# Linear attention and an MLP mixer on one core: fp32 dummy matmuls, halves in one product, and a later place for q's transposes

## Chip, cores and metric

The kernel runs on one core of a Trainium2 chip. The metric is the device time of one execution in microseconds, as the median over runs. All ratios are computed as the mean time of one kernel's fast runs over the mean of the other's fast runs of the same rounds, so they are not quite the ratio of the medians quoted beside them. The 95% interval of a ratio stands in brackets.

## The reference

```python
def _attn_ref(q, k, v):                    # 8 batches, 8 heads, 576 rows, head size 64
    phi = lambda x: np.where(x > 0, x, np.exp(x) - 1.0) + 1.0
    q_p, k_p = phi(q), phi(k)
    kv = np.einsum('bhsd,bhse->bhde', k_p, v)
    z = np.sum(k_p, axis=2)
    num = np.einsum('bhsd,bhde->bhse', q_p, kv)
    den = np.einsum('bhsd,bhd->bhs', q_p, z)[..., None] + 1e-06
    return num / den
# the heads side by side give x: 8 x 576 x 512
def _moe_ref(x, w_tok1, w_tok2, w_ch1, w_ch2):
    h = np.maximum(x.transpose(0, 2, 1) @ w_tok1, 0.0) @ w_tok2
    u = x + h.transpose(0, 2, 1)
    return u + np.maximum(u @ w_ch1, 0.0) @ w_ch2
```

## The kernel before: the parts that matter here

The instructions of each engine stand in program order. Batch 0 is done by itself in the opening, about the first 25 us; every later batch is prepared beside the channel matmuls of the one before. In the opening the order on TensorE is: dummies; the transposes of batch 0's first half of q; the column sums of k; two more dummies; the first kv product; the second half's transposes; the numerators; the second kv; then the first token product, 20 matmuls that stand in the profile as L427.

phi(k) is kept as a sum of two terms, kr = max(k, 0) and kp = min(exp(k), 1), so every kv product has two terms.

```python
    def kv_first(c, copy):
        ps = sm_tile()[:, :, 0:2 * D]
        for k_ in (kr, kp):
            for t in range(T):
                on, off = k_ is kr and t == 0, k_ is kp and t == T - 1
                if c == 0:                                   # halves: 2 matmuls of 64x128 by 128 columns
                    for a in range(2):
                        nc.tensor.matmul(out=ps[:, a], lhsT=k_[half[a], c, t],
                                         rhs=v0[half[a], 2 * c:2 * c + 2, t], start=on, stop=off)
                else:                                        # quarters: 4 matmuls of 64x64 by 64 columns
                    for a, i in QUARTERS:
                        nc.tensor.matmul(out=ps[half[i], a, 0:D], lhsT=k_[half[a], c, t, i],
                                         rhs=v0[half[a], 2 * c + i, t], start=on, stop=off)
        ...                                                  # two copies into kvbd

    def warm(m):                                             # dummies: 128x512 bf16
        ps = bank()
        for _ in range(m):
            nc.tensor.matmul(out=ps, lhsT=identity, rhs=identity[:, None, :].to_broadcast([128, 4, 128]),
                             start=True, stop=True)

    def tick(m):                                             # dummies of one column
        ps = sm_tile()
        for k_ in range(m):
            a, i = QUARTERS[k_ % 4]
            nc.tensor.matmul(out=ps[half[i], a, 0:1], lhsT=identity[half[a], 0:64],
                             rhs=identity[half[a], 0:1], start=True, stop=True)
    ...                                                      # cut: loads and memsets
    nc.gpsimd.memset(w1t, 0.0)
    nc.gpsimd.memset(qT[0], 0.0)
    nc.vector.memset(qT[1], 0.0)
    for c in range(2):
        load_v0(c)                                           # v of batch 0, issued by GpSimd
    ...
    for m in (100, 52, 52):
        tick(m)
        warm(4)
    k_first(0, 1)
    ...                                                      # cut
    warm(2)
    kv_first(0, act)
    ...
    # batch 1's q transposes ("qt0", "qt1") and products, by the index of the big group they follow;
    # groups 3 to 11 are mm3 (w_ch1), from 12 on they are blocks of four matmuls on w_ch2
    at0 = {"qt0": 11, "qt1": 13, "vc": 13, "kv": 14, "nd00": 15, ...}
```

## Time and profile before

| | before |
|---|---|
| median of 3 runs | 265.81 us (265.56 to 266.7) |
| span of the profiled run | 264.0 us |
| TensorE busy | 256.9 us, 97% |
| TensorE's first real work | 9.68 us |
| first kv product starts | 11.96 us |
| start of the 36 matmuls that carry on without a break at w_ch1 | 26.48 us |
| idle before batch 1's q transposes | 0.5 us |

In the order of time a row gives the start and the length in us, the engine, the source line, the operation, what it wrote and read, how many instructions were merged, and in brackets the idle time before it with what ended it ("issue" means that nothing the profile shows was waited for). In the chain that ended last a piece has only start, length, engine, tile, line and count. The lines themselves are in the prediction below.

### The profile page before, as it was taken

How to read it: one execution, taken by the hardware profiler on the slowest of the kernel's cores; microseconds unless marked ns; L12 is line 12 of the kernel's file. 1: busy time of each engine (PE TensorE's matmuls, PEld its weight loads, DVE VectorE, ACT ScalarE, POOL GpSimd, SP SyncE). 2: the span in 40 equal slices, each digit the busy share in tenths (PEclk: the TensorE clock that was granted, in tenths of full speed). 3: DMA queues.
4: the chain of work that ended last, by engine and by line, in shares of the span. 5: the costliest groups of instructions: out<-in, count | busy, mean ns of one | idle time of the engine just before them, and what ended most of it. 6: DMA issues, size and time to landing. Idle time of an engine off the chain costs nothing.

```text
span 264.0 us, 5626 instructions
## 1 busy us (share of the span) xinstructions
PE 256.9 (97%) x2344; PEld 136.0 (52%) x2344; DVE 158.6 (60%) x312; ACT 133.0 (50%) x204; POOL 33.5 (13%) x54
## 2 busy tenths in 40 slices
PE   7999999999999999999999999999999999999994
PEld 4685445554744454455554554455554554444642
DVE  5755977967829786948684286938684272420122
ACT  4564878268455358425870358435870354027300
POOL 9730300020002300030001300030001300000000
PEclk9999999999999999999999999999999999999999
DMA  7999999499505996599999991671066500740043
GB/s 252 251 203 274 376 220 391 155 197 370 206 2 113 190 337 266 121 248 386 271 402 178 261 405 65 147 163 42 2 130 120 120 1 2 148 110 0 2 99 100
DMA packets 50089, 48.37 MB, mean 183 GB/s; under 512 B 30288, under 2 KB 35536, under 8 KB 50064
## 3 DMA queue, kind: packets, MB, share of 16 engines
q1 hardware_dynamic: 41904, 35.53, 45.7%
q0 software_dynamic: 7440, 11.44, 20.9%
q10 hardware_dynamic: 720, 1.05, 1.3%
q8 instruction: 18, 0.29, 0.4%
q14 instruction: 7, 0.06, 0.1%
HBM read 35.85 MB, written 9.44 MB: 172 GB/s over the span
## 4 chain that ended last, share of the span: by engine, by line
PE 95%; ACT 1%; DVE 1%; issue 1%; POOL 0%; ACTq 0%; POOLq 0%
PE h_ps L515 33%; PE c_ps L489 32%; PE a_ps L248 6%; PE h_ps L261 5%; PE c_ps L503 4%; PE nd_ps L210 3%; PE bank L573 2%; PE kv_ps L169 2%; PE bank L581 1%; PE h_ps L552 1%; PE bank L427 1%; PE bank L180 1%; PE bank L438 1%; PE bank L392 1%; DVE u L440 0%
## 5 line engine op out<-in xcount | busy, mean ns | idle before, releaser
L496 ACT ACTIVATE cr<-c_ps 128x512 bf16<-128x512 f32 x91 | 53.4, 599 | 76.4 <-PE c_ps L489 76.2
L489 PE MATMUL c_ps<-uT,wc 128*128 128x512 bf16 x384 | 91.5, 379 | 0.0
L515 PE MATMUL h_ps<-wc,cr 128*128 128x512 bf16 x372 | 84.9, 379 | 0.0
L515 PEld LDWEIGHTS <-cr 128*128 128x128 bf16 x372 | 36.0, 98 | 41.3
L489 PEld LDWEIGHTS <-wc 128*128 128x128 bf16 x384 | 35.7, 98 | 36.4 <-issue 0.9
L532 DVE TENSOR_TENSOR o_sb<-h_ps,u 128x512 f32<-128x512 f32 x31 | 21.1, 689 | 23.1 <-PE h_ps L515 23.0
L537 POOL DMA_DIRECT2D out_dram<-o_sb x24 | 14.9, 626 | 153.5 <-DVE o_sb L532 153.5
L222 DVE TENSOR_TENSOR x<-nd_ps,den 128x512 bf16<-128x512 f32 (+1 forms) x42 | 25.3, 603 | 1.5
L139 DVE TENSOR_SCALAR e<-e 128x1152 bf16<-128x1152 bf16 x30 | 13.9, 464 | 12.6 <-ACT e L125 12.5
L273 DVE TENSOR_TENSOR u<-h_ps,x 128x1024 bf16<-128x1024 f32 x12 | 14.3, 1219 | 10.1 <-PE h_ps L261 10.1
L125 ACT ACTIVATE e<-k_raw 128x1152 bf16<-128x1152 f32 x16 | 18.7, 1169 | 2.5 <-DMA k_raw<-in_k_dram 2.5
L125 ACT ACTIVATE e<-q_raw 128x1152 bf16<-128x1152 f32 x16 | 18.4, 1160 | 1.8 <-DMA q_raw<-in_q_dram 1.8
L219 DVE TENSOR_SCALAR den<-nd_ps 128x8 f32<-128x8 f32 (+1 forms) x42 | 6.9, 164 | 18.6 <-PE nd_ps L210 17.9
L210 PEld LDWEIGHTS <-qT 128*128 128x128 bf16 x140 | 11.4, 98 | 9.3 <-issue 0.2
L261 PE MATMUL h_ps<-ar,w2p 128*128 128x512 bf16 x60 | 16.0, 379 | 0.1
L210 PE MATMUL nd_ps<-kvbd,qT 128*128 128x130 bf16 x140 | 15.1, 223 | 0.0
L251 ACT ACTIVATE ar<-a_ps 128x512 bf16<-128x512 f32 x14 | 7.6, 594 | 13.7 <-PE a_ps L248 13.7
L248 PE MATMUL a_ps<-x,w 128*128 128x512 bf16 x56 | 14.4, 379 | 0.0
L542 DVE TENSOR_TENSOR o_sb<-h_ps,ut 128x512 f32<-128x512 f32 x4 | 2.8, 689 | 18.7 <-PE h_ps L515 18.7
L151 ACT CAST vs<-v_raw 128x1152 bf16<-128x1152 f32 x12 | 13.9, 1159 | 0.0
L131 DVE TENSOR_SCALAR y<-q_raw 128x1152 bf16<-128x1152 f32 x16 | 12.4, 775 | 0.6 <-DMA q_raw<-in_q_dram 0.3
L140 DVE TENSOR_TENSOR qp<-e,y 128x1152 bf16<-128x1152 bf16 x16 | 12.1, 758 | 0.6
(112 smaller groups left out, 226.4 us busy)
## 6 DMA issues: line engine op xcount, KB each, us to landing
k_raw<-in_k_dram SPq DMA_DIRECT2D x16, 576.0 KB, 9.0
q_raw<-in_q_dram SPq DMA_DIRECT2D x16, 576.0 KB, 7.8
v_raw<-in_v_dram SPq DMA_DIRECT2D x14, 576.0 KB, 11.0
out_dram<-o_sb POOLq DMA_DIRECT2D x24, 256.0 KB, 4.6
wc<-in_moe_w_ch_dram POOLq DMA_DIRECT2D x8, 384.0 KB, 9.7
out_dram<-o_sb SPq DMA_DIRECT2D x9, 128.0 KB, 2.3
out_dram<-o_sb ACTq DMA_DIRECT2D x7, 128.0 KB, 2.6
out_dram<-o_sb POOLq DMA_DIRECT2D x6, 128.0 KB, 5.9
```

What stands on the lines that cost most here:

```text
L125: nc.scalar.activation(out=e, in_=f, func=AF.Exp)
L139: nc.vector.tensor_scalar(out=e, in0=e, scalar1=1.0, scalar2=None, op0=ALU.min)
L210: nc.tensor.matmul(out=o[:, a], lhsT=qT[b][:, t0:t0 + 128], rhs=kvbd[b][:, c, a], start=True, stop=True)
L222: nc.vector.tensor_tensor(out=x[b][:, rs[0]:rs[0] + m, HG * D * g:HG * D * (g + 1)].rearrange("p r (h d) -> p r h d", h=HG), in0=v_[:, :, ...
L248: nc.tensor.matmul(out=ps[:, mt], lhsT=w1t[:, b, ms] if r == R else w1[:, r, ms], rhs=x[b][:, r, :], start=(r == 0), stop=(r == R))
L261: nc.tensor.matmul(out=ps[:, i], lhsT=w2v(kt, r, b), rhs=ar[b][:, kt, :], start=(kt == 0), stop=(kt == NT - 1 and not add))
L273: nc.vector.tensor_tensor(out=u[b][:, rs[0]:rs[0] + m], in0=ps[:, 0:m], in1=x[b][:, rs[0]:rs[0] + m], op=ALU.add)
L489: nc.tensor.matmul(out=ps, lhsT=wc1[:, kj, 128 * mc:128 * mc + 128], rhs=uT[b][:, :, kj], start=(kj == 0), stop=(kj == NDM - 1))
L496: nc.scalar.activation(out=cr[b][:, mc, :], in_=ps, func=AF.Relu)
L515: nc.tensor.matmul(out=ps, lhsT=crt[:, kc, :] if t == 8 else cr[b][:, kc, 128 * r:128 * r + 128], rhs=wc2[:, kc, :], start=(kc == 0), stop ...
L532: nc.vector.tensor_tensor(out=o, in0=ps, in1=u[b][:, r, :], op=ALU.add)
L537: (nc.scalar if last and e else put).dma_start(out=outv[2 * p + b, :, 2 * r0 + e:2 * r0 + e + 2 * m - 1:2], in_=live["o"][half[e], 0:m])
```

## The change

Three parts. The dummies become four fp32 matmuls of 512 columns on a zeroed tile and one of 256 columns later, in place of 204 one-column ticks and 14 bf16 matmuls. In batch 0's second kv only the second term stays on quarters; the first goes to halves. And batch 1's q transposes move one block further behind the first rows of w_ch2. The intent is to have the clock up by a few long instructions, and to take a wait off TensorE. The diff:

```diff
--- before.py
+++ after.py
@@ -361,18 +361,19 @@
         for k_ in (kr, kp):
             for t in range(T):
                 on, off = k_ is kr and t == 0, k_ is kp and t == T - 1
-                if c == 0:
+                if c == 0 or k_ is kr:
                     for a in range(2):
                         nc.tensor.matmul(out=ps[:, a], lhsT=k_[half[a], c, t],
-                                         rhs=v0[half[a], 2 * c:2 * c + 2, t], start=on, stop=off)
+                                         rhs=v0[half[a], 2 * c:2 * c + 2, t],
+                                         start=on, stop=off)
                 else:
                     for a, i in QUARTERS:
-                        nc.tensor.matmul(out=ps[half[i], a, 0:D], lhsT=k_[half[a], c, t, i],
+                        nc.tensor.matmul(out=ps[half[i], a, i * D:(i + 1) * D],
+                                         lhsT=k_[half[a], c, t, i],
                                          rhs=v0[half[a], 2 * c + i, t], start=on, stop=off)
         for i in range(2):
-            at = 0 if c else i * D
             copy(out=kvbd[0][half[i], c, :, i * D1:(i + 1) * D1 - 1],
-                 in_=ps[half[i], :, at:at + D])
+                 in_=ps[half[i], :, i * D:(i + 1) * D])
 
     def q_cols(r, a, c):
         t0 = D * (T * (2 * a + c) + 2 * r)
@@ -567,23 +568,19 @@
                 for g in range(2):
                     load(nm, n, g)
 
-    def warm(m):
+
+    zeros = raw["v", 1].rearrange("p j f -> p (j f)")[:, 0:512]
+
+    def warm(m, cols=512):
         ps = bank()
         for _ in range(m):
-            nc.tensor.matmul(out=ps, lhsT=identity, rhs=identity[:, None, :].to_broadcast([128, 4, 128]),
+            nc.tensor.matmul(out=ps[:, 0:cols], lhsT=zeros[:, 0:128], rhs=zeros[:, 0:cols],
                              start=True, stop=True)
-
-    def tick(m):
-
-        ps = sm_tile()
-        for k_ in range(m):
-            a, i = QUARTERS[k_ % 4]
-            nc.tensor.matmul(out=ps[half[i], a, 0:1], lhsT=identity[half[a], 0:64],
-                             rhs=identity[half[a], 0:1], start=True, stop=True)
 
 
     landed = {}
     one = work.tile([128, 1], FP32, name="one", tag="one", bufs=1)
+    nc.vector.memset(zeros, 0.0)
     nc.vector.memset(one, 0.0)
     nc.scalar.activation(out=one, in_=one, func=AF.Exp)
     for c, nms in enumerate(("kq", "qk")):
@@ -628,9 +625,7 @@
     dve, act = nc.vector.tensor_copy, nc.scalar.copy
     e_first("k", 0)
     k_first(0, 0)
-    for m in (100, 52, 52):
-        tick(m)
-        warm(4)
+    warm(4)
     k_first(0, 1)
     e_first("q", 0)
     q_first(0, 0)
@@ -643,7 +638,7 @@
     qput_first(0, 1, act)
     ksum_first(0, act)
     e_first("k", 1)
-    warm(2)
+    warm(1, 256)
     kv_first(0, act)
     k_first(1, 0)
     qtr_first(1)
@@ -726,7 +721,7 @@
     big = [lambda mc=mc: mm3(0, mc, range(2, 4)) for mc in range(3)] + \
         [lambda mc=mc: mm3(0, mc, dve=mc in (3, 6, 9)) for mc in range(3, NCH)] + \
         [lambda kc=kc: m4_0(kc) for kc in range(NCH)]
-    at0 = {"qt0": 11, "qt1": 13, "vc": 13, "kv": 14, "nd00": 15, "nd01": 16, "nd10": 17,
+    at0 = {"qt0": 12, "qt1": 14, "vc": 13, "kv": 14, "nd00": 15, "nd01": 16, "nd10": 17,
            "nd11": 18, "nd20": 19, "nd21": 20, "mm1": 21}
     fill = [(2, mm2_first_tail)]
     for ex, ad, en, nm, c in ((2, 2, 3, "k", 0), (5, 5, 6, "k", 1), (8, 8, 9, "q", 0),
```

## The prediction

> **What bounds the kernel now.** I read the head of the profile page first, then the chain that ended last over the first 45 us, then the order of time over the first 17 us and around 34 us, and last the loads that the opening waits for. Quoted below, in that order: two lines of the page; pieces of the chain (start in us, length in us, what); rows in order of time; and one load's row with its time to landing.
>
> ```profile
> PE 256.9 (97%) x2344; PEld 136.0 (52%) x2344; DVE 158.6 (60%) x312; ACT 133.0 (50%) x204; POOL 33.5 (13%) x54
> PEclk9999999999999999999999999999999999999999
> ...
> 2.86 1.82 PE bank L573 x4
> 4.68 0.79 PE bank L581 x27
> ...
> 8.07 1.82 PE bank L573 x4
> 9.89 0.96 PE bank L180 x9
> ...
> 12.03 1.11 PE bank L366 x36
> ...
> 15.02 0.75 PE bank L370 x72
> ...
> 26.48 7.89 PE c_ps L489 x36
> ...
> 34.42 0.47 issue
> ...
> 7.79 0.76 DVE L140 TENSOR_TENSOR qp<-e,y 128x1152 bf16<-128x1152 bf16 x1
> ...
> 9.68 1.17 PE L180 MATMUL bank<-identity,qp 128*128 128x128 bf16 x9
> ...
> 11.17 0.86 PE L573 MATMUL bank<-identity 128*128 128x512 bf16 x2
> ...
> 11.96 0.68 PE L366 MATMUL bank<-cr,kr 64*128 64x128 bf16 x18
> ...
> 34.05 0.76 DVE L140 TENSOR_TENSOR qp<-e,y 128x1152 bf16<-128x1152 bf16 x1
> ...
> 34.86 0.34 PE L180 MATMUL tp<-identity,qp 128*128 128x128 bf16 x3 [0.51 <-DVE qp L140]
> ...
> L117 POOL DMA_DIRECT2D cr<-in_v_dram x1: 852/852/852, 3.7 to 3.7; - x1
> ...
> DMA to landing us min/median/max: 7.9/7.9/7.9
> ```
>
> TensorE is the bound: 256.9 of 264.0 us busy, and the chain is almost wholly its work. What can be won is only what TensorE does needlessly, slowly or waiting. The rows show three places.
>
> First, the opening. Until 9.89 us TensorE does only dummy work (L581 one-column ticks, L573 128x512 dummies). A group of four L573 takes 1.82 us, so about 0.43 us from start to start, while 36 real matmuls of the same 512 columns later take 7.89 us, 0.22 us each. So TensorE ran at half speed, though the PEclk row shows 9 in every slice: that row does not show this slowness. The first nine transposes took 1.17 us; the same nine take 0.68 us at 13.1 us. The two dummies at 11.17 took 0.86 us together, and everything behind them is at full speed: full speed came only at about 11.4 us. The operand of the transposes (L140 qp) was ready at 7.79+0.76 = 8.55, but dummies already in the queue held them until 9.68.
>
> Second, what the first real product (L366) needs: v's first half, issued at 3.73 us and landed 7.9 us later, near 11.63. It began at 11.96. So the opening is bound by a load, not by the transposes or dummies, apart from the last 0.3 us.
>
> Third, at 34.4 us TensorE idles for 0.5 us: the transposes of batch 1's q stand before the first rows of w_ch2, and their operand comes at 34.05+0.76 = 34.81.
>
> [...]
>
> [...]
>
> [...]
>
> **The change part by part.**
>
> Dummies. 204 ticks and 12 + 2 bf16 dummies go; four fp32 dummies of 512 columns come at the start and one of 256 columns before the first kv. They read a zeroed tile, so VectorE gets one more memset of 128x512 fp32. Its memset of 128x1184 four-byte elements took 1.04 us, so this takes about 0.45 us, from 0.8 to 1.3. Its other memsets end 0.45 us later, at about 3.6 instead of 3.16; its first real work waits for k until 4.70, so this is hidden. The dummies then start near 1.35, as the ticks did. [...] So the transposes begin at about 8.6 (1.1 us earlier) and take 0.68 instead of 1.17 us; the sums behind take 0.46[...]: TensorE is free at about 10.2 us. Then it waits for v at 11.63. Of the 1.8 us gained ahead of the product only 11.96 - 11.70 = 0.26 us survives (0.06 us from landing to start, as after the first k: it landed at 0.74 + 3.9 = 4.64, and work began at 4.70). ScalarE and VectorE move earlier too, but k's second half lands only at 2.28 + 9.1 = 11.4, and its exp began at 11.79, so those gain at most 0.4 us. Worth: -0.25 us.
>
> The second group of kv. Its first term goes from 36 quarter matmuls to 18 halves; only its second term stays on quarters. From the chain, 36 halves took 1.11 us (0.031 each) and 72 quarters 0.75 us (0.0104 each). So the first term goes from 36 x 0.0104 = 0.375 to 18 x 0.031 = 0.555 us: +0.18 us[...]. It is on the path, since the copies of kvbd and the next products wait for its end at 15.77 (the second half of v is no limit: it landed by 13.6). Worth: +0.2 us. The copies read as many elements as before.
>
> q's transposes of batch 1. The order of instructions on TensorE shows the four matmuls of the first row block of w_ch2 now ahead of the first nine transposes, and three blocks ahead of the second nine, before kv. Four such matmuls take 0.86 us. They begin at 34.42, when the last c_ps matmul is done; the fourth needs the accumulator that ScalarE empties by 34.40+0.60 = 35.0, and is due at 34.42 + 3 x 0.215 = 35.07, so it just doesn't wait. The transposes then begin at about 35.3, after qp at 34.81. The wait of 0.5 us goes, and so does a wait of 0.06 us before the second nine. Behind, kv needs v's cast (over at 38.17) and would come at about 38.3; nd comes at 40.0 instead of 40.5. The weights allow this: the second part of w_ch2 lands at 30.76 + 6.3 = 37.1, and its first use comes near 39. TensorE's remaining idle gaps after this are only tenths, so the gain reaches the end. Worth: -0.55 us.
>
> Sum: -0.25 + 0.2 - 0.55 = -0.6 us. [...]before, full speed could come later than in this profile (its runs spread from 265.56 to 266.7, over 1 us), which the changed kernel should mostly be spared; I put 0.1 us on that. 265.81 - 0.7 = 265.1 us.
>
> **The rivals.** (a) The clock falls back. [...] For it: about 70% did not wake the clock before. [...] I give it one in six.
> (b) The opening gains nothing because the v load moves. If the extra memset slows GpSimd's memsets ahead of that load, v lands 0.1 to 0.3 us later: about 265.5. GpSimd's rates (1.0 ns an element beside VectorE's memsets, 0.87 later) speak for a small effect.
> (c) The opening gains much more, 1 to 2 us, because the transposes set the path: 264. The landing of v at 11.63 speaks against it.
> (d) The order at 34 us gives nothing, as ScalarE (3.66 of 4 us busy there) becomes the bound for v's cast and the copies: 265.7.
>
> **Range and chances.** 265.1 us, with 264.3 to 266.5 holding it 8 times in 10: below, the sum without the cost of halves and with a better start; above, (b) with (d) or a mild (a). Two per cent is 5.3 us, more than any part could give, so within 2% is 0.97, faster 0.015, slower 0.015.
>
> **What would show it.** [...]the first transposes at 8.6 with 0.68 us for nine; an idle TensorE before the first kv at about 11.7; the halves of the second kv 0.2 us longer; no wait before the transposes near 35. If the first kv matmuls take twice their spacing, (a) is true. If the first kv starts well before 11.6 or after 12, my reading of the v load is wrong. If the gap at 34 us is only replaced by one before kv or nd, (d) holds.

The sum came to -0.25 + 0.2 - 0.55 = -0.6 us, with the allowance for timed runs -0.7 us, so 265.1 us. Terms behind it: the time of the four fp32 dummies and of the last one (which stood between 8.6 + 0.68 + 0.46 = 9.74 us and the 10.2 us at which TensorE is free), the time at which the clock comes up, and a small cost of the switch from halves to quarters on top of the 0.18 us. That the clock is up by the first transposes is an estimate without a ground shown here, and so is the size of rival (a). The 70% in rival (a) is measured: in the kernel before, the groups of four dummies start at 2.86, 5.46 and 8.07 us, 2.6 us apart, and each takes 1.82 us; the clock came to full only at 11.75 us. In the trace of the changed kernel the four fp32 dummies take 5.88 us and the last one 0.68 us.

## The result, and the profile after

The changed kernel took 264.44 us (264.21 to 264.61, 4 runs) where before took 265.99 us (265.56 to 266.7, 4 runs): ratio 0.9939 [0.9914, 0.9963]. The profiled run's span is 262.4 us. Run again later, on another occasion, it took 264.91 us (263.72 to 266.37, 6 runs) beside 265.7: ratio 0.9968 [0.9940, 0.9996]. So the gain is clear of noise in both, in the second only just, and somewhere between 0.85 and 1.6 us.

The page's line of busy time for the changed kernel, then pieces of its chain, then its rows in order of time:

```profile
PE 254.2 (97%) x2118; PEld 134.1 (51%) x2118; DVE 159.1 (61%) x313; ACT 133.3 (51%) x204; POOL 33.5 (13%) x54
```

```profile
3.73 6.58 DMA cr<-in_v_dram
10.36 1.18 PE bank L366 x36
...
13.42 0.61 PE bank L366 x18
14.03 0.45 PE bank L371 x36
...
15.82 2.18 PE bank L428 x20
...
25.19 7.89 PE c_ps L490 x36
```

```profile
1.46 5.88 PE L577 MATMUL bank<-v_raw 128*128 128x512 f32 x8 [1.46 <-DVE ones L590]
...
5.03 0.34 PEld L577 LDWEIGHTS bank<-v_raw 128*128 128x128 f32 x1 [0.52 <-issue]
5.89 0.19 PEld L577 LDWEIGHTS bank<-v_raw 128*128 128x128 f32 x1 [0.52 <-issue]
6.32 0.19 PEld L577 LDWEIGHTS bank<-v_raw 128*128 128x128 f32 x1 [0.24 <-issue]
...
8.46 0.68 PE L180 MATMUL bank<-identity,qp 128*128 128x128 bf16 x9 [1.12 <-DVE qp L140]
...
32.91 1.22 PE L516 MATMUL h_ps<-wc,cr 128*128 128x512 bf16 x4
33.07 0.76 DVE L140 TENSOR_TENSOR qp<-e,y 128x1152 bf16<-128x1152 bf16 x1
...
33.97 0.66 PE L180 MATMUL tp<-identity,qp 128*128 128x128 bf16 x9
```

And the row that ends the view of v's first load in the changed kernel, as it stood for the kernel before with 7.9:

```profile
DMA to landing us min/median/max: 6.6/6.6/6.6
```

What to see, from the top. The four fp32 dummies are eight rows, two to an instruction; the weight loads come 0.86 us apart (5.03 to 5.89) and then 0.43 us apart (5.89 to 6.32). So the clock doubles near 5.9 us. The trace keeps its own record of the granted clock, which begins when the clock comes to full (the page's PEclk row counts the time ahead of the record as full): it begins at 5.89 us here and at 11.75 us in the kernel before. The transposes start at 8.46, as soon as their operand is there (1.12 us idle before them), and take 0.68 us instead of 1.17. The chain no longer runs through dummies but through v's load, which landed 6.6 us after its issue, not 7.9; the first kv starts at 10.36 instead of about 12.0. The second kv takes 0.61 + 0.45 = 1.06 us instead of 0.75. The long run of w_ch1 starts 26.48 - 25.19 = 1.29 us earlier. At 33 us the block of w_ch2 fills the gap, and no wait is left before the transposes. In the chain the first product behind them (L210) began at 40.60 before and at 38.70 now: 1.90 us, 1.29 from the opening and 0.61 from the new order. Some 0.3 us of it is given back later (spans 264.0 and 262.4); a wait of 0.2 us for a transposing transfer of the u tail is part of that, the rest I did not trace.

### The profile page after: what moved, and what is told of

Its sections match the earlier page's. It is cut to its first block, busy times and chain, and to the rows that moved or that the text cites. A ratio compares the mean times of both kernels' runs of the same rounds, so it can differ in the third digit from the quotient of the medians.

```text
span 262.4 us, 5175 instructions
## 1 busy us (share of the span) xinstructions
PE 254.2 (97%) x2118; PEld 134.1 (51%) x2118; DVE 159.1 (61%) x313; ACT 133.3 (51%) x204; POOL 33.5 (13%) x54
## 4 chain that ended last, share of the span: by engine, by line
PE 87%; DMA 7%; ACT 2%; POOL 1%; DVE 1%; issue 1%; ACTq 0%; POOLq 0%
PE h_ps L516 33%; PE c_ps L490 29%; PE a_ps L248 5%; PE h_ps L261 5%; DMA uTt<-ut 4%; PE c_ps L504 4%; PE nd_ps L210 3%; DMA cr<-in_v_dram 3%; PE kv_ps L169 2%; PE h_ps L553 1%; PE bank L428 1%; POOL qT L597 1%; PE bank L366 1%; PE bank L439 1%; PE bank L393 1%
## 5 line engine op out<-in xcount | busy, mean ns | idle before, releaser
L210 PEld LDWEIGHTS <-qT 128*128 128x128 bf16 x140 | 11.4, 98 | 9.3 <-issue 0.2
L210 PE MATMUL nd_ps<-kvbd,qT 128*128 128x130 bf16 x140 | 15.1, 223 | 0.0
L251 ACT ACTIVATE ar<-a_ps 128x512 bf16<-128x512 f32 x14 | 7.6, 595 | 11.4 <-PE a_ps L248 11.4
## 6 DMA issues: line engine op xcount, KB each, us to landing
v_raw<-in_v_dram SPq DMA_DIRECT2D x14, 576.0 KB, 10.8
```

The lines of the kernel that those rows point to most:

```text
L210: nc.tensor.matmul(out=o[:, a], lhsT=qT[b][:, t0:t0 + 128], rhs=kvbd[b][:, c, a], start=True, stop=True)
```

## The experiments

Twelve kernels ran, all with correct results. Each job also ran the kernel before on the same chip, and ratios are to that. State is fast wherever nothing is said.

| kernel | median us | before beside it | ratio to before | first kv starts | v's first half, issue to landing | 36 matmuls of first kv | clock full from |
|---|---|---|---|---|---|---|---|
| before | - | - | 1 | 12.0 | 7.9 | 1.11 | 11.75 |
| changed | 264.44 | 265.99 | 0.9939 | 10.4 | 6.6 | 1.18 | 5.89 |
| changed, again | 264.91 | 265.70 | 0.9968 | 10.9 | 7.1 | 1.18 | 5.28 |
| order alone | 265.59 | 266.28 | 0.9973 | 12.2 | 8.0 | 1.44 | 12.84 |
| dummies alone | 265.83 | 266.28 | 0.9986 | 11.0 | 7.2 | 1.18 | 7.14 |
| halves alone | 266.84 | 265.70 | 1.0035 | 12.2 | 7.8 | 1.83 | 13.67 |
| changed without halves | 265.34 | 266.28 | 0.9966 | 11.6 | 7.8 | 1.18 | 6.91 |
| ticks put back | 266.04 | 266.28 | 0.9997 | 12.9 | 7.4 | 1.62 | 13.98 |
| 18 ticks added | 264.93 | 265.70 | 0.9981 | 11.0 | 7.2 | 1.18 | 7.25 |
| bf16 dummies | 264.38 | 265.70 | 0.9949 | 10.9 | 7.1 | 1.18 | 5.22 |
| no dummies | 266.16 | 265.93 | 1.0006 | (slow profile) | | |  |
| 456 ticks | 276.81 | 265.93 | 1.0419 | 21.9 | 7.9 | 2.04 | 25.45 |
| v first | 268.83 | 265.93 | 1.0089 | 10.2 | 8.6 | 1.18 | 5.66 |
| v first, bf16 dummies | 268.81 | 265.93 | 1.0078 | 10.1 | 8.4 | 1.18 | 6.33 |

The last four columns are of the one profiled run of each, and are in us; the last is where the trace's record of the granted clock begins. The two kernels with v first issue v's load at 1.5 us, all others at 3.7.

The theory to begin with (A): v lands earlier because the ticks are gone. The trace of before has a packet of 16 KB on a queue that the profile lists as "instruction" (q8) at 5.71 us, which took 0.97 us in the midst of the loads; in the changed kernel the first such packet is at 15.22 us. The rival (B): the early landing was chance.

### Order alone

```diff
-    at0 = {"qt0": 11, "qt1": 13, "vc": 13, ...}
+    at0 = {"qt0": 12, "qt1": 14, "vc": 13, ...}
```

> Before, with only q's transposes of batch 1 moved behind the first rows of w_ch2. If the wait of 0.5 us before those transposes is simply removed: 0.55 to 0.6 us faster than before (about 265.4), the opening unchanged (first kv at about 12 us, v's first half 7.9 us from issue to landing). Rival, that ScalarE or the cast of v takes its place: no gain beyond 0.2 us.

Measured: 265.59 us, ratio 0.9973 [0.9956, 0.9990], so 0.7 us. In its profile the block of w_ch2 comes before the transposes with no wait:

```profile
34.68 1.23 PE L515 MATMUL h_ps<-wc,cr 128*128 128x512 bf16 x4
35.74 0.66 PE L180 MATMUL tp<-identity,qp 128*128 128x128 bf16 x9
```

The opening is as before: first kv at 12.18 and v's landing at 8.0 us from issue. The order gains what the wait was worth, and the gain reaches the end. ScalarE did not become a new bound.

### Dummies alone

The edit is the part of the diff above from the zeroed tile to the second dummy, without the kv and the order.

> Before, with only the dummy work changed to five fp32 matmuls. Theory A (the load of v and the second halves of k and q land earlier because TensorE's shorter program needs no instruction fetch of 16 KB at about 6 us): v lands 6.6 us after issue instead of 7.9, no instruction packet before 12 us, gain 1.4 to 1.7 us (about 264.4). Theory B (the landing in the changed kernel's profile was chance): landing stays near 7.9 us, gain at most 0.3 us.

Measured: 265.83 us, ratio 0.9986 [0.9970, 1.0003]: a quarter of what theory A expected of the time, and not clear of noise. Part of A's picture is there: no instruction packet before 15.70 us, v landing after 7.2 us, the first kv at 10.98. But the next experiment and this one show where the rest went.

### The changed kernel without halves

```diff
-                if c == 0 or k_ is kr:
+                if c == 0:
```

> The changed kernel with both terms of the second group's kv back on quarters. If halves cost what their spacing says (36 x 0.010 against 18 x 0.031 us[...]): 0.2 to 0.35 us faster than the changed kernel, about 1.85 us faster than before. Rival: the 36 more instructions bring the next instruction fetch earlier, into w_tok's or w_ch1's loads, and the gain is lost: equal to the changed kernel.

Measured: 265.34 us, ratio 0.9966 [0.9945, 0.9987]: not faster than the changed kernel, though not told apart from its second measurement either (0.9968). The order of time shows why the cheaper quarters do not pay. First the kernel with the dummies alone, then this one:

```profile
17.06 0.27 PE L427 MATMUL bank<-x,w 128*128 128x256 bf16 x1
18.08 0.94 PE L427 MATMUL bank<-x,w 128*128 128x256 bf16 x7 [0.75 <-issue]
```

```profile
17.65 0.27 PE L427 MATMUL bank<-x,w 128*128 128x256 bf16 x1
18.59 0.94 PE L427 MATMUL bank<-x,w 128*128 128x256 bf16 x7 [0.67 <-issue]
```

In both, TensorE pauses for 0.7 us between the eleventh and twelfth matmul of the first token product, waiting for nothing that the profile names. The changed kernel runs all 20 in one piece. The packet records suggest a reason: an instruction packet of 16 KB starts at 15.70 in the one kernel and at 16.20 in the other, and TensorE resumes 2.38 and 2.39 us after that. Both have 36 more instructions ahead of this point than the changed kernel, because 36 quarters with 36 weight loads stand where 18 halves with 18 weight loads do. This gives theory C, which is my reading and not a row of the trace: TensorE ran out of program here, and the halves pay back the 0.3 us that they cost by moving that point behind the arrival of the next piece.

The landing of v is 7.8 us here though no instruction packet came before 16 us, which speaks against A as the whole story.

### Ticks put back

```diff
-    warm(4)
+    for m in (100, 52, 52):
+        tick(m)
+        warm(1)
```

> The changed kernel with the 204 one-column ticks put back between three of the fp32 dummies, so that TensorE has again some 400 more instructions in the opening and is just about as busy. Theory A (instruction fetch): a 16 KB instruction packet at about 6 us again, v's first half again 7.9 us from issue to landing, first kv at about 12 us, the time 1.2 to 1.7 us above the changed kernel, so at most 0.6 us better than before. Theory B (chance, or something else in the fp32 dummies or the zeroed tile frees the load): landing stays at 6.6 us and first kv at about 10.4.

Measured: 266.04 us, ratio 0.9997 [0.9979, 1.0015]: the whole gain is gone, the order's 0.7 us too. The instruction packet is back at 6.23 us; v landed after 7.4 us, between the two theories. What set the end of the opening was something else:

```profile
12.93 1.62 PE bank L366 x36
```

Ticks and fp32 dummies at half clock (one's two rows took 2.08 us together) filled TensorE until 10.25 us, so the transposes came late and at half speed (1.17 us for nine), and the first kv began at 12.93, long after v, and part of it at half speed. By the trace's record the clock came up only at 13.98 us. So the ticks did harm here: they occupied TensorE without bringing the clock up. (This kernel also has three fp32 dummies ahead of the transposes, not four.)

### The changed kernel again, with 18 ticks, with bf16 dummies, and halves alone

The yardstick:

> The changed kernel itself, run again beside the next three on one chip, for the scatter of the landing of v and as their yardstick. If its profile was typical: 1.4 to 1.7 us faster than before, v's first half 6.6 to 7.2 us from issue to landing, no pause of TensorE among the 20 matmuls of batch 0's first token product. If its landing was a lucky draw: 7.2 to 8 us, and about 1 us faster than before.

Measured: 0.9968 [0.9940, 0.9996], v's landing 7.1 us, no pause. The landing of the first profile, 6.6 us, was at the good end, and single runs lay between 263.72 and 266.37.

18 ticks, as a call of the tick helper behind the four dummies:

> The changed kernel with 18 one-column ticks (36 instructions) behind the four fp32 dummies, where TensorE is idle for over 1 us, so they cost no time themselves. Theory C (the two experiments with the second kv on quarters paused 0.65 us for want of instructions, since 36 more instructions stand ahead of the point where the next 16 KB of program must have come): the pause returns at the same place, the twelfth matmul of batch 0's first token product, 0.6 to 0.75 us, and the kernel is 0.5 to 0.8 us slower than the changed one. Rival (the pause belongs to the quarters[...]): no pause, time equal to the changed kernel within 0.1 us.

Measured: 264.93 us, ratio 0.9981 [0.9962, 1.0000]: perhaps 0.35 us slower than the changed kernel, within the noise. The pause is there, at the very place, but short. This is the row of weight loads, the one ahead of the twelfth matmul:

```profile
17.57 0.66 PEld L428 LDWEIGHTS <-w 128*128 128x128 bf16 x7 [0.23 <-issue]
```

The instruction packet started at 15.19 here, and 17.57 is again 2.38 us later; in the other two kernels it started closer to the point of need. So theory C holds for the place and for the delay from packet to resumption. What was wrong is the size, because the packet's start also moves. The rival, that quarters themselves pause, falls: this kernel has the halves.

Halves alone, on the kernel before:

> Before, with only the first term of the second kv on halves. Theory C says that halves are worth something only where they move a program boundary; before had no such pause, so here they only cost: second kv 1.06 us instead of 0.75, and the kernel 0.2 to 0.4 us slower than before. Rival, halves gain by themselves: faster than before.

Measured: 266.84 us, ratio 1.0035 [1.0020, 1.0050]: 0.9 us slower, more than expected. The chain:

```profile
12.18 1.83 PE bank L366 x36
...
15.89 0.61 PE bank L366 x18
16.50 0.45 PE bank L371 x36
```

The second kv takes 1.06 us instead of 0.75, as expected: 0.31 us. In this profile the first kv also took 1.83 us where before had 1.11 and the order alone 1.44, although the opening up to there is the same program in all three. This is the clock coming up later in one execution than in another: its record begins at 13.67 us here, at 12.84 in the order alone and at 11.75 in before. The first kv had then run 1.49 and 0.66 us at half clock; half of that on top of 1.11 makes 1.85 and 1.44. Whether that explains the other 0.6 us of the timed runs (five of six at 266.65 to 266.9, one at 265.81) stays open.

bf16 dummies:

```diff
-            nc.tensor.matmul(out=ps[:, 0:cols], lhsT=zeros[:, 0:128], rhs=zeros[:, 0:cols],
+            nc.tensor.matmul(out=ps, lhsT=identity, rhs=identity[:, None, :].to_broadcast([128, 4, 128]),
-    nc.vector.memset(zeros, 0.0)
-    warm(4)
+    warm(16)
-    warm(1, 256)
+    warm(2)
```

> The changed kernel with its dummies as 16 and 2 bf16 matmuls of 512 columns on the identity, and no zeroed tile: the same time on TensorE (16 x 0.43 = 6.8 us cold), 34 more matmul and weight-load rows where the fp32 ones have a few each. If fp32 matters only as a short way to write busy time: full speed at the same 5 to 8 us, no pause, or one of at most 0.5 us near the end of the first token product since the program is longer; time within 0.4 us of the changed kernel. Rival, that fp32 passes wake the clock better: first kv and transposes at half speed, over 0.5 us slower.

Measured: 264.38 us, ratio 0.9949 [0.9935, 0.9962]: the same as the changed kernel. The dummies take 5.5 us, the transposes 0.68, the first kv 1.18, and there is no pause. No gain from fp32 as such shows here; unbroken dummies of either type do the same (full clock from 5.22 us here, from 5.28 and 5.89 with fp32).

### No dummies, 456 ticks, and v's load first

No dummies at all in the changed kernel (both calls removed):

> The changed kernel without any dummy matmul. If the dummies only serve to have the clock at full speed for the first real work: the first transposes take 1.17 us instead of 0.68 and the first kv's 36 halves 1.8 to 2.2 us instead of 1.18, [...]1.5 to 3 us slower than the changed kernel, that is 0 to 1.5 us slower than before. Rival, the dummies are not needed: equal to the changed kernel.

Measured: fast runs 1.0006 [0.9986, 1.0026] of before, so 0.4 to 0.7%, 1.0 to 1.8 us, above the two measurements of the changed kernel, which are of other jobs: the dummies are needed. Its profile fell in a run of 269.72 us that counts as slow, so I read nothing more from it.

456 ticks in place of the four dummies:

> The changed kernel with 456 one-column ticks in place of the four fp32 dummies[...]. Theory A (instruction fetches in the opening delay the loads): two or three instruction packets between 3 and 11 us, v's first half lands 8.5 us or more from issue, k's second half over 9.5 us. Rival (the scatter of the landings, 6.6 to 8.0 so far, has nothing to do with fetches): 6.6 to 7.8 us. The time is a poor guide here, since ticks do not wake the clock (first transposes and kv at half speed expected): 265.5 to 268.

Measured: 276.81 us, ratio 1.0419, far outside what I expected.

```profile
1.36 3.15 PE L586 MATMUL bank<-identity 64*64 64x1 bf16 x223 [1.36 <-POOL identity masks.py:199]
8.49 1.87 PE L586 MATMUL bank<-identity 64*64 64x1 bf16 x128 [3.98 <-issue]
14.68 1.55 PE L586 MATMUL bank<-identity 64*64 64x1 bf16 x105 [4.33 <-issue]
```

TensorE executes 223 ticks with their weight loads, 446 instructions, and stops for 3.98 us; then 128 more, exactly 256 instructions, and stops for 4.33 us; after the next 256 it stops a third time, for 2.94 us. This is theory C at its plainest. The instruction packets start at 6.30, 12.30 and 18.39 us, about 6.0 us apart; each carries 16 KB, and TensorE resumes 2.2 to 2.4 us after its start. The first stop comes after as many instructions in the three kernels that paused in the first token product: the traces have 446 rows of matmul and weight load ahead of the pause in the dummies alone, in the kernel without halves and in the one with 18 ticks (447 here, with one weight load more). The clock's record begins only at 25.45 us.

Because TensorE stood still so long, only one instruction packet fell among the loads, not two or three, so the experiment is a poor test of theory A: v landed after 7.9 us, k's second half after 8.8. Taken together, the five kernels with an instruction packet near 6 us had v's landing at 7.9, 8.0, 7.8, 7.4 and 7.9 (mean 7.8), and the six fast profiles without one at 6.6, 7.1, 7.2, 7.8, 7.2 and 7.1 (mean 7.2). In the trace of before one set of packets of k's second half trails until 11.0 us, one every 0.19 us, long after the others; in the changed kernel the last is over at 9.1. I took this for a hold-up by the 16 KB packet. But the changed kernel without halves, which has no such packet before 16.20 us and landed at 7.8, shows two such trains, also until 11.0 us, so the trail does not tell; packets are not labelled by engine, and no kernel differs in that packet alone. So A is supported on average by 0.6 us and not proven.

v's loads ahead of GpSimd's two memsets:

```diff
+    for c in range(2):
+        load_v0(c)
     nc.gpsimd.memset(w1t, 0.0)
     nc.gpsimd.memset(qT[0], 0.0)
     nc.vector.memset(qT[1], 0.0)
-    for c in range(2):
-        load_v0(c)
```

> The changed kernel with GpSimd issuing the two loads of v before its two long memsets (issue at about 1.3 us instead of 3.73). If the landing of v is what bounds the opening: it lands before 10 us, the first kv starts at about 10.0, right behind the last dummy (in the profiles of the changed kernel 10.4 and 10.9), with nothing left of the wait for v, and the time is 0.3 to 0.9 us below the changed kernel. Rival, the second halves of q and k pay for it[...]: transposes start 0.5 us or more later, no gain.

> The kernel with 18 bf16 dummies, with v's loads ahead of GpSimd's memsets: the candidate for the best version. The same gain as in the other v-first kernel: 0.3 to 0.9 us below the bf16-dummy kernel, so 263.5 to 264 us where before has 265.8.

Measured: 1.0089 [1.0052, 1.0126] and 1.0078 [1.0030, 1.0125]: slower. Most runs lie near 265.5 or near 269 us, with 266.12 and 267.48 between; one of 270.0 counts as slow and is left out of the ratio. The first kv did start at 10.2 and 10.1 us as expected, with no wait for v. But the loads of q and k paid for it. In the first of the two, k's second half, in the view of that load, and the rows that follow:

```profile
DMA to landing us min/median/max: 10.8/10.8/10.8
```

```profile
14.92 0.74 PE L393 MATMUL bank<-kvbd,qT 128*128 128x128 bf16 x10 [1.49 <-ACT kvbd L375]
...
16.17 1.14 PE L366 MATMUL bank<-cr,kr 64*128 64x128 bf16 x18
```

k's second half landed 10.8 us after issue, where the changed kernel had 7.1 and 7.5. Its exp on ScalarE was late, and a copy that stands behind it in ScalarE's queue held TensorE up for 1.49 us. And the 18 halves after the waits took 1.14 us instead of 0.68: the clock had fallen back, and the 20 matmuls of the first token product took 3.67 us instead of 2.18. The profile of the second kernel waited too (1.3 us) but kept its clock, and there they took 2.18 us. The view by stretches shows the fall: a row gives start and end, length, then busy time and number of rows of TensorE, its weight loads, VectorE, ScalarE and GpSimd, then the granted clock, and DMA. First two rows of the kernel that fell back, then one of the other:

```profile
12.00:16.00 4.00, 2.00 (x44) 1.84 (x45) 2.46 (x6) 2.80 (x5) 2.09 (x3) 0.99 1.31 202
16.00:20.00 4.00, 3.73 (x85) 3.28 (x83) 1.96 (x5) 1.08 (x6) 0.00 (x0) 0.50 1.32 204
```

```profile
12.00:16.00 4.00, 2.75 (x100) 2.53 (x97) 3.01 (x6) 3.19 (x7) 2.10 (x3) 1.00 1.31 204
```

By the trace's record the clock was at half from 15.90 to 22.72 us. So rival (a) of the prediction can happen. The share of busy time alone does not say when: TensorE was busy 2.00 and 2.75 of these 4 us, but only 1.77 of the 4 us from 6.92 to 10.92 in the repeat of the changed kernel, and there the clock stayed up. Why it fell stays open. Each timed run has its mean granted clock, and it divides the two groups: 0.984 to 0.987 in all eight runs of 268.58 us and more, 0.997 to 1.000 in the four below. The 6.83 us at half clock would lower the mean by 0.013. Neither is a better version. I have none that clearly beats the changed kernel; the bf16 dummies equal it.

## Why the prediction was right, and which terms were not

The measured 264.44 us lies in the predicted range, near its lower end, and the change stayed far within 2%. Part of that is luck: the first profile's landing of v was the earliest of all, and the second measurement gives 0.85 us instead of 1.6. By the prediction's own steps:

- **The order at 34 us: -0.55 us.** Right. The profiles give 0.61, the kernel with this part alone 0.7 (0.27%).
- **The clock.** Right: full speed at 5.9 us, and between 5.2 and 7.3 in all eight profiles with unbroken dummies, though the reckoning behind it is cut, since no run here shows the rule that it used (for the kernel before I read 11.4 off the dummies; the trace's record says 11.75, which changes no sum); transposes 0.68 us at 8.46 (predicted 8.6); an fp32 dummy of 512 columns took 1.71 us at half clock (two rows of 0.855 us), four times the 0.43 us of a bf16 one. In every fast profile with unbroken dummies the first kv took 1.18 us, and where ticks were used 1.11 to 2.04: the moment of the clock's rise, for which I allowed 0.1 us, was worth up to 0.7 us in a single run.
- **The first kv, -0.25 us.** The mis-sized term. I took v's landing of 11.63 us as fixed. It measured 6.6 and 7.1 us from issue instead of 7.9, and the first kv began at 10.36 and 10.91, so 1.6 and 1.1 us earlier than before. By the prediction's own sign, a start well before 11.6, its reading of v's load was wrong; why v lands earlier is not proven. That the opening was bound by v was right: TensorE waited for v after the last dummy, 0.25 and 0.91 us.
- **The halves, +0.2 us.** The cost itself measured 0.31 us. What I missed is what else they do: without them TensorE paused 0.67 us in the first token product. I did not count instructions.
- **Rivals.** (a) did not occur in the two profiles of the changed kernel, but it did in the one with v's load first. (One timed run of the changed kernel, 266.37 us, has a granted clock of 0.992, the lowest of its ten; no profile shows why.) (b): the extra memset did not move GpSimd, which issued v's load at 3.73 in both. (c), that the transposes set the path and the opening gains 1 to 2 us, was near in size and wrong in cause. (d) did not occur.

The parts do not add up: order -0.27%, dummies -0.14% and halves +0.35% alone sum to -0.06%, the whole measured -0.61% and -0.32%. The pause can explain 0.28% of the gap of 0.26 to 0.55%: the dummies alone suffer it (0.75 us), and the halves cost by themselves but remove it. The three parts were run in two jobs, and 0.6 us of what the halves alone cost is unexplained, so the sum is no closer than that.

## What to carry to other kernels

Count the instructions ahead of a busy stretch, not only their time: here a TensorE program of many tiny matmuls stopped after 446 instructions for 3.98 us and after the next 256 for 4.33 us, until 2.2 to 2.4 us after a packet of instructions began, and the stop stands in the profile only as an idle "issue". Where dummies are needed to bring the clock up, use a few long ones: 5.5 us and more of unbroken dummies had it up between 5.2 and 7.3 us in eight profiles, while dummies for about 70% of each period, with one-column ticks between, left it low until 11.75 us. And before moving a load forward, see which load it will push back: in this opening k's second half became the new wait (landed 10.8 us after issue instead of 7.1 and 7.5). The landings scatter too: the same 288 KB load, issued at 3.7 us, landed 6.6 to 8.0 us later over these kernels, which is over 1 us on a path that waits for it.
